# Batch 2's queries and keys by a half-precision copy and transposed loads, with a new written order of the front

## The chip, the cores and the metric

The kernel runs on one core of a Trainium2 chip. The metric is the device time of one execution in microseconds (us), lower is better: the median of three runs. Beside it stands one profiled execution with its trace. PE is the matrix engine, DVE the vector engine, ACT the scalar engine, POOL and SP the two engines that issue nearly all DMAs here.

## The reference

Eight batches of twelve heads go through an attention whose softmax has one more term in its denominator; the result, head by head in a row, goes through two matrix products with a squared ReLU between them. In float32:

```python
batch, n_heads, seq, head_dim = (8, 12, 448, 64)
scores = scale * np.matmul(q, k.transpose(0, 1, 3, 2))
m = np.max(scores, axis=-1, keepdims=True)
e = np.exp(scores - m)
attn = e / (np.sum(e, axis=-1, keepdims=True) + np.exp(-m) + 1e-09)
attn_out = np.matmul(attn, v)
x = attn_out.transpose(0, 2, 1, 3).reshape(B * S, H * D)     # 3584 x 768
h = x @ w_in                                                 # 768 x 2048
r = np.maximum(h, 0.0)
out = (r * r) @ w_out                                        # 2048 x 768
```

## The kernel before

All matrix products run in half precision. The written order of steps is what each engine gets: `manual_schedule` is on, each engine and each DMA queue takes its steps in the order of the string, and an engine waits where data or a buffer is not there yet. A step is a letter with numbers. `ORDER` is the front, run once; `CYCLE` is run twice, for batches 4 and 5 and for batches 6 and 7 (`period(b)` with b = 4 and 6); then a plain loop does the last two batches of the two matrix products.

What the letters mean, as far as they are needed:

- `s` scores of 64 keys of a quad (four heads) into one of two PSUM buffers, `e` the exponential of them on ACT, `a` the sums on DVE, `S` `Z` `M` the denominator, `v` the products with the values (`p`, `b`, `y`, `z`, `n`, `x` are the like for batch 0, which is done in halves), `X` the division that writes a quad of the transposed attention output `xt`.
- `j` two or six of the six partial products of a tile (128 of 2048 columns) of the first layer, `k` the ReLU, `l` the square. In the front `j0` to `j15` are batch 1's tiles and `j16` to `j31` batch 0's; `i` is a pair of tiles of half of batch 0.
- `o` pieces of the second layer for 128 tokens and half the columns, `O` and `Q` its two steps out of PSUM; `Q` also issues the store on SP.
- `d` a load from the list `LOADS` (in `CYCLE`, of `following`).

There are two ways by which a batch's queries and keys get into the tile `qk` with the head dimension on the partitions. Batches in `ON_PE` (line 37) are loaded on POOL in natural layout as half precision (`load_quad`, tile `nn`), transposed by PE (`T`, 14 transposes for a quad's queries or keys) into PSUM, and copied to `qk` by DVE or ACT (`U`). The others are staged: POOL issues two DMAs that copy q and k to DRAM as half precision (`stage`), SP issues three DMA transposes of 128 x 2688 elements out of that copy (`transposed_load`: queries, keys, and keys shifted by one position), and POOL copies the last keys of each head into a tile of their own (`tail_keys`). The scores of a staged batch need all three planes. They are made by eight matmuls of 224 columns in place of four of 448, and the rows of the output then lie in the store in steps of 2 and not of 7.

`qk`, the value tile `vn` and the tail keys have two buffers each, so batch b waits for batch b-2 to be done with them. The tile `ot` of a finished output piece has five buffers; one comes free when its store has landed. DMAs that POOL issues are in one hardware queue (q0 of the profile), those that SP issues in another (q1). Of each kind at most eight are under way, since each waits for the one eight before it.

In the front before the change, batches 0, 1 and 2 are transposed by PE and only batch 3 is staged; batch 4 is staged there too. The weights `win` (four loads of two DMAs) and `wout` (four DMAs) come in on the same POOL queue.

Of the kernel before, what the change touches and what calls it, by code (L numbers as in the profile page):

```python
# [16 lines left out]
def kernel(  # L17
# [17 lines left out]
    NQ = H // 4  # L35
    KC = S // 64
    ON_PE = (0, 1, 2)
# [21 lines left out]
    osb_pool = ctx.enter_context(tc.tile_pool(name="osb", bufs=5))  # L59
# [103 lines left out]
    def transposed_load(b, i):  # L163
        qk = qk_of(b)
        n, x, c = PLANES[i]
        nc.sync.dma_start(
            out=qk[:, i, 0:c],
            in_=stages[n, b][x:x + c * 2 * D].rearrange("(r c) -> r c", c=2 * D),
            transpose=True,
        )  # L170
# [501 lines left out]
    def other_ring():  # L672
# [4 lines left out]
        d0 W8 d8 d1 c1,4,0 c0,0,1 t0,0,0 c1,0,1 t1,0,0 u0,0,0,0 t1,0,4 u1,0,0,0 c0,4,1 u1,0,4,1 t0,0,4 d2 s0 t0,1,0 u0,0,4,1 u0,1,0,0 t1,1,0 u1,1,0,0  # L677
        d10 d9 s1 t0,1,4 e0 t1,1,4 e1 s2 e2 u0,1,4,0 s12 e12 u1,1,4,0 T0,1,0 T0,1,1 U0,1,0,0,4,0 U0,1,1,0,4,0 U0,1,1,4,7,0 U0,1,0,4,7,0 s3 s4 p2 p0 e3
        b0,0 e4 s6 p1 d18 p3 s5 e6 e5 b0,1 b0,2 T0,2,0 b0,3 y0 T0,2,1 U0,2,0,0,4,0 z0 n0 U0,2,1,0,4,0 b1,0 s8 U0,2,0,4,7,0 U0,2,1,4,7,0 x0 d3 d17 d16
        b1,1 s9 d15 T1,0,1 e8 e9 U1,0,1,0,7,0 T1,0,0 U1,0,0,0,7,0 b2,0 s11 e11 s10 s13 e10 e13 s14 p8 b2,1 p4 d5 b2,2 p9 s7 e14 p10 b2,3 p11 y2 p5 e7  # L680
        z2 b1,2 p6 s15 b1,3 p7 e15 y1 b3,0 n2 x2 b3,1 z1 s17 e17 b3,2 p12 p13 b3,3 n1 s18 p14 s16 e18 p15 x1 y3 T1,1,0 U1,1,0,0,7,0 e16 b4,0 z3 b4,1
        s19 e19 i0,6 n3 r0,6,0 s20 e20 s21 i0,7 s22 x3 b4,2 e21 p16 b4,3 e22 b5,0 r0,7,0 p17 p18 p19 d4 b5,1 g0,6 y4 z4 n4 s23 T1,1,1 e23 d13 s27 b5,2
        x4 i0,4 s28 p20 p21 g0,7 b5,3 e27 p22 p23 y5 U1,1,1,0,7,0 e28 z5 r0,4,0 n5 x5 s26 s29 e26 j20,0,2 j23,0,2 j23,2,4 j20,2,4 j20,4,6 e29 j23,4,6
        s25 k23,1 s24 g0,4 e25 e24 k20,0 P0 i1,7 j19,0,2 l23 a0,0 s32 e32 a0,1 s36 d6 j19,2,4 e36 j16,0,2 l20 j19,4,6 j17,0,2 s34 s33 k19,1 r1,7,0
# [4 lines left out]
        v1,0 v1,1 v1,2 v1,3 v1,4 d23 v1,5 k26,1 v1,6 a2,0 a2,1 a2,2 s44 s47 M1 l26 e44 j21,2,4 d22 j21,4,6 i1,4 X1 a2,3 k21,1 v2,0 v2,1 v2,2 r1,4,0 S2
        e47 v2,3 Z2 v2,4 v2,5 l21 v2,6 M2 o0,0,4 s46 o0,4,8 d14 s50 e46 e50 o0,8,12 X2 o0,12,16 s51 g1,4 s48 O0,1 Q0 j15,0,2 j0,0,2 j15,2,4 j4,0,2  # L690
        j15,4,6 j4,2,4 j4,4,6 j0,2,4 e51 e48 j0,4,6 s45 k15,1 l15 o2,0,4 s49 e45 e49 o2,4,8 s52 d21 o2,8,12 a3,0 e52 o2,12,16 k4,1 k0,0 s53 a3,1 s55
        d24 j10,0,2 O2,1 j1,0,2 Q2 j10,2,4 j1,2,4 j10,4,6 l0 j14,0,2 l4 j1,4,6 j11,0,2 e55 k10,0 j14,2,4 a3,2 j11,2,4 k1,1 j8,0,2 l10 j14,4,6 j11,4,6
# [4 lines left out]
        j13,4,6 l5 a5,2 j3,0,2 j3,2,4 j3,4,6 k12,0 a5,3 s69 l12 k6,1 o3,0,4 l6 k13,1 k3,1 l3 S5 l13 o3,4,8 o3,8,12 o3,12,16 O3,0 Q3 e69 s70 Z5 s71 d26
        M5 v5,0 v5,1 v5,2 v5,3 e70 e71 v5,4 v5,5 v5,6 o9,0,2 o9,2,4 X5 o9,4,6 o9,6,8 s66 o9,8,10 s68 o9,10,12 o9,12,14 o9,14,16 e66 O9,0 o6,0,2 e68
        s67 s72 o6,2,4 o6,4,6 o6,6,8 e67 o6,8,10 Q9 a6,0 a6,1 e72 a6,2 s73 o8,0,2 o6,10,12 o6,12,14 o8,2,4 o6,14,16 s75 e73 O6,0 o8,4,6 o8,6,8 e75 s78
        Q6 o8,8,10 o8,10,12 a6,3 e78 o8,12,14 s79 o8,14,16 s77 v6,0 v6,1 v6,2 v6,3 e79 e77 v6,4 S6 v6,5 v6,6 Z6 M6 s74 O8,0 Q8 o7,0,2 o7,2,4 e74 X6  # L700
        o7,4,6 s76 e76 a7,0 o7,6,8 o7,8,10 o7,10,12 o7,12,14 a7,1 o7,14,16 s82 d28 o10,0,2 O7,1 o10,2,4 o10,4,6 Q7 o10,6,8 s80 a7,2 e82 o10,8,10
        o10,10,12 o10,12,14 o10,14,16 e80 s85 s83 o11,0,2 o11,2,4 e85 o11,4,6 o11,6,8 d31 O10,1 Q10 e83 s81 a7,3 d29 o11,8,10 o11,10,12 o11,12,14 e81
        o11,14,16 O11,1 Q11 s84 o12,0,2 s86 o12,2,4 o12,4,6 e84 e86 o12,6,8 o12,8,10 a8,0 o12,10,12 o12,12,14 o12,14,16 S7 a8,1 O12,0 o13,0,4 o13,4,8
        d30 o13,8,12 Z7 Q12 a8,2 o13,12,16 v7,0 v7,1 v7,2 v7,3 O13,1 v7,4 a8,3 v7,5 v7,6 M7 S8 Q13 v8,0 v8,1 Z8 v8,2 v8,3 M8 v8,4 v8,5 X7 v8,6 X8
# [7 lines left out]
    def period(b):  # L712
# [3 lines left out]
        def following(n):  # L716
            ahead, what = ((1, n) if n < 6 else (2, 6) if n < 7 else (1, 6) if n < 8 else (2, n - 8))
            t = b + ahead
            if t < B and (n != 7 or b > FIRST_PERIOD):
                if what < 3:  # L720
                    transposed_load(t, what)
                elif what < 5:
                    tail_keys(t, (what - 2,))
                elif what == 5:
                    load_v_quads(t)
                else:
                    stage(t)
# [98 lines left out]
```

## Time and profile before

| what | value |
|---|---|
| time, median of 3 runs (all three) | 392.37 us (391.68 to 394.08) |
| the profiled execution, its own time | 392.36 us |
| its span in the profile | 390.6 us |
| instructions | 14257 |
| DMA packets | 75052, 45.34 MB |
| POOL's queue q0 | 24752 packets, 22.62 MB, 37.6% of 16 engines' span |
| SP's queue q1 | 49952 packets, 21.59 MB, 28.6% |
| transposed loads of queries, 5 | median 6.2 us from issue to landing |
| transposed loads of keys, 10 | median 7.1 us |
| loads of `wout`, 4 of 768 KB | median 15.3 us |
| copies of q to DRAM, 4 of 676 KB | median 14.0 us |

Lines of the profile are read as follows. A group of instructions has its line in the kernel, engine, operation, output and inputs, shape and count; then its busy time, the mean duration of one in ns, and the engine's idle time before it with what ended it. Lines 93 and 254 are helpers (`mm` and `exp`), so the tiles tell the steps apart. The duration of one matmul has its latency in it, and up to four matmuls run side by side in quarters of the array, so a busy PE need not be a full one. `DMA` in tenths is the mean busy share of the 16 DMA engines.

### The profile page before, as it was taken

The page shows a single profiled execution, that of the slowest core. Times are in us where ns is not written, and L with a number is a line of the kernel's source. Part 1 is how long each engine was busy: PE and PEld are TensorE (multiplying, and loading weights), DVE is VectorE, ACT ScalarE, POOL GpSimd, SP SyncE. Part 2 cuts the span into 40 slices and gives each one's busy share as a digit, 9 for nine tenths or more (in the row PEclk, how much of TensorE's full clock was granted, in tenths as well). Part 3 has the DMA queues.
Part 4 walks back from the last instruction along what each step waited for, and adds up shares of the span by engine and source line. Part 5 has one row for each costly group of instructions (what it writes and reads, how often), then busy time and mean ns, then how long its engine had stood idle before and what let it go on. Part 6 is the DMA issues. An engine that isn't in the chain of part 4 may idle for free.

```text
span 390.6 us, 14257 instructions
## 1 busy us (share of the span) xinstructions
PE 381.8 (98%) x6432; PEld 254.3 (65%) x6432; DVE 253.5 (65%) x468; ACT 228.3 (58%) x308; POOL 61.9 (16%) x96
## 2 busy tenths in 40 slices
PE   9689999999999999999999999999999999999997
PEld 5566656565689865567777665567777755556665
DVE  3887995765765766556968757575878788880000
ACT  5999998586689611249989731248988720001221
POOL 8443420025000700410001240210000000000000
PEclk9999999999999999999999999999999999999999
DMA  8999999999939899903129697901112200001132
GB/s 144 204 204 205 201 199 206 159 203 176 215 84 166 168 186 118 201 2 66 44 59 196 148 178 156 165 4 44 60 48 64 64 23 2 0 0 62 61 82 81
DMA packets 75052, 45.34 MB, mean 116 GB/s; under 512 B 47472, under 2 KB 72944, under 8 KB 74992
## 3 DMA queue, kind: packets, MB, share of 16 engines
q0 software_dynamic: 24752, 22.62, 37.6%
q1 hardware_dynamic: 49952, 21.59, 28.6%
q8 instruction: 50, 0.82, 1.0%
q10 hardware_dynamic: 288, 0.23, 0.2%
q14 instruction: 10, 0.08, 0.1%
HBM read 45.69 MB, written 17.93 MB: 163 GB/s over the span
## 4 chain that ended last, share of the span: by engine, by line
PE 89%; ACT 5%; DMA 2%; DVE 2%; POOL 1%; issue 1%; POOLq 0%; DVEq 0%; ACTq 0%
PE mp L93 79%; PE sp L93 8%; ACT et L254 3%; DMA nn<-in_k_dram 2%; PE mp L207 1%; POOL nn L117 1%; ACT rcp L372 1%; ACT rcp L365 0%; DVE half L441 0%; DVE xt L487 0%; DVE half L443 0%; DVE half L445 0%; ACT rcp L466 0%; ACT rcp L463 0%; DVE half L447 0%
## 5 line engine op out<-in xcount | busy, mean ns | idle before, releaser
L93 PE MATMUL mp<-wout,gs 64*64 64x384 f16 (+2 forms) x2928 | 165.4, 322 | 0.0
L93 PE MATMUL mp<-xt,win 128*64 128x448 f16 (+2 forms) x1188 | 148.3, 347 | 0.1
L93 PEld LDWEIGHTS <-gs 64*64 64x64 f16 (+1 forms) x2928 | 103.8, 106 | 33.9
L93 PEld LDWEIGHTS <-win 128*64 128x64 f16 (+1 forms) x1188 | 83.2, 106 | 63.5 <-issue 4.2
L254 ACT ACTIVATE et<-sp 128x896 f16<-128x896 f32 (+2 forms) x131 | 110.6, 891 | 12.7 <-PE sp L93 12.2
L505 DVE TENSOR_SCALAR rt<-mp 128x448 f16<-128x448 f32 x87 | 54.0, 622 | 15.9 <-PE mp L93 12.9
L509 DVE TENSOR_TENSOR gs<-rt 128x448 f16<-128x448 f16 x128 | 49.4, 404 | 21.9 <-ACT rt L503 20.0
L503 ACT ACTIVATE rt<-mp 128x448 f16<-128x448 f32 x41 | 21.8, 543 | 64.9 <-PE mp L93 50.9
L575 ACT ACTIVATE ot<-mp 128x384 f32<-128x384 f32 (+2 forms) x31 | 14.9, 480 | 70.5 <-PE mp L93 70.4
L93 PE MATMUL sp<-qk 64*64 64x224 f16 (+1 forms) x1056 | 53.3, 274 | 1.9 <-ACT et L254 1.2
L93 PEld LDWEIGHTS <-qk 64*64 64x64 f16 x1056 | 32.8, 114 | 14.3 <-issue 5.7
L188 POOL COPY flatq<-qk 64x384 f16<-64x384 f16 x20 | 14.5, 724 | 169.6 <-DMA qk<-stage_k 169.1
L254 ACT ACTIVATE nn<-sp 128x896 f16<-128x896 f32 x42 | 37.1, 916 | 4.3 <-PE sp L93 4.2
L487 DVE TENSOR_TENSOR xt<-mp,rcp 128x448 f16<-128x448 f32 x42 | 24.3, 620 | 15.6 <-ACT rcp L466 10.0
L581 DVE SCALAR_TENSOR_TENSOR ot<-mp,ot 128x384 f32<-128x384 f32 x42 | 23.4, 557 | 14.0 <-ACT ot L575 11.5
L93 PEld LDWEIGHTS <-vn 64*64 64x64 f16 x756 | 22.5, 107 | 9.8 <-issue 1.4
L93 PE MATMUL mp<-et,vn 64*64 64x448 f16 (+1 forms) x448 | 24.5, 343 | 0.0
L577 DVE TENSOR_SCALAR ot<-mp 128x384 f32<-128x384 f32 x26 | 14.4, 555 | 15.1 <-PE mp L93 14.9
L463 ACT ACTIVATE rcp<-sp,one_b 128x896 f32<-128x896 f32 x21 | 21.1, 1007 | 3.3 <-PE sp L93 3.3
L466 ACT ACTIVATE rcp<-rcp 128x896 f32<-128x896 f32 x21 | 19.9, 949 | 0.5
L441 DVE TENSOR_TENSOR half<-et 128x1792 f16<-128x1792 f16 x15 | 16.5, 1100 | 4.3 <-ACT et L254 4.2
L443 DVE TENSOR_TENSOR half<-half,et 128x1792 f16<-128x1792 f16 x15 | 16.3, 1087 | 0.3
(59 smaller groups left out, 195.7 us busy)
## 6 DMA issues: line engine op xcount, KB each, us to landing
out_dram<-ot SPq DMA_DIRECT2D x52, 96.0 KB, 2.4
out_dram<-ot SPq DMA_DIRECT2D x19, 192.0 KB, 1.9
win<-in_moe_w_in_dram POOLq DMA_DIRECT2D x8, 384.0 KB, 12.3
wout<-in_moe_w_out_dram POOLq DMA_DIRECT2D x4, 768.0 KB, 15.3
vn<-in_v_dram POOLq DMA_DIRECT2D x10, 288.0 KB, 7.9
stage_q<-in_q_dram POOLq DMA_DIRECT2D x4, 676.0 KB, 14.0
stage_k<-in_k_dram POOLq DMA_DIRECT2D x4, 676.0 KB, 16.7
nn<-in_q_dram POOLq DMA_DIRECT2D x8, 224.0 KB, 8.9
```

Of the source, the lines that this page charges most:

```text
L93: return nc.tensor.matmul(out_, lhsT, rhs, start=start, stop=stop)
L254: nc.scalar.activation(out=out_, in_=in_, func=AF.Exp, scale=scale)
L441: nc.vector.tensor_add(esq[m], a[:, 0:w], a[:, w:2 * w])
L443: nc.vector.tensor_add(esq[m], esq[m], z[:, 0:w])
L463: nc.scalar.activation(out=rcp, in_=zp[:, :, 0:S], func=AF.Ln, bias=one_b)
L466: nc.scalar.activation(out=zqs[m], in_=zqs[m], func=AF.Exp, scale=-1.0)
L487: nc.vector.tensor_mul(xts[b][:, 2 * g + i, :], xqs[m][i][:, 0:S], zqs[m][:, i, :])
L503: nc.scalar.activation(out=rt[:, 0:m], in_=hp[:, 0:m], func=AF.Relu)
L505: nc.vector.tensor_scalar(out=rt[:, 0:m], in0=hp[:, 0:m], scalar1=0.0, scalar2=None, op0=ALU.max)
L509: nc.vector.tensor_mul(gs[:, f0:f0 + per, t0 % RING:t0 % RING + n], r, r)
L575: nc.scalar.activation(out=ot, in_=op[:, 0:w], func=AF.Copy, scale=OUT_SCALE)
L581: nc.vector.scalar_tensor_tensor(out=ot, in0=lo[:, 0:w], scalar=OUT_SCALE, in1=ot, op0=ALU.mult, op1=ALU.add)
```

## The change

Four things change. Batch 2 leaves `ON_PE`: its 84 transposes on PE and six copies out of PSUM go, and it is staged, loaded transposed, and its tail keys copied, as batch 3 is. The order string of the front is a new one: the first layer of batch 0 lies beside the attention of batch 1, then comes the first layer of batch 1 as a block, and then the attention of batches 2 and 3 beside the second layer. The loads move: in the front only batches 2 and 3 are staged; a cycle that begins with batch b stages and loads b and b+1, where before it loaded b+1 and b+2. And `ot` has eight buffers.

```diff
-    ON_PE = (0, 1, 2)
+    ON_PE = (0, 1)
...
-    osb_pool = ctx.enter_context(tc.tile_pool(name="osb", bufs=5))
+    osb_pool = ctx.enter_context(tc.tile_pool(name="osb", bufs=8))
...
-        x = {(0, 1): (0, 0), (0, 2): (0, 1), (1, 0): (1, 0), (1, 1): (0, 0), (1, 2): (0, 1),
-             (2, 0): (1, 0), (2, 1): (1, 1), (2, 2): (0, 0)}[b, g]
+        x = {(0, 1): (0, 0), (0, 2): (0, 1), (1, 0): (1, 0), (1, 1): (0, 0), (1, 2): (0, 1)}[b, g]
...
-    LOADS = ([lambda b=b, g=g: load_quad(b, g) for b in range(3) for g in range(NQ) if b + g]
+    LOADS = ([lambda b=b, g=g: load_quad(b, g) for b in range(2) for g in range(NQ) if b + g]
              + [lambda b=b, g=g: load_v_quads(b, g, g + 1) for b in range(2) for g in range(NQ)]
-             + [lambda: load_v_quads(2)]
              + [lambda i=i: load_win(i, NW) for i in range(NW)]
-             + [lambda n0=n0, y=y: load_wout(n0, y, 2) for n0 in (0, HALF) for y in range(2)]
-             + [lambda: stage(3), lambda: transposed_loads(3), lambda: tail_keys(3), lambda: load_v_quads(3),
-                lambda: stage(4), lambda: transposed_loads(4), lambda: tail_keys(4), lambda: load_v_quads(4), lambda: stage(5)])
+             + [lambda n0=n0, y=y: load_wout(n0, y, 2) for n0 in (0, HALF) for y in range(2)])
+    for b in (2, 3):
+        LOADS += [lambda b=b: stage(b), lambda b=b: load_v_quads(b)]
+        LOADS += [lambda b=b, i=i: transposed_load(b, i) for i in range(3)]
+        LOADS += [lambda b=b, i=i: tail_keys(b, (i,)) for i in (1, 2)]
...
-            ahead, what = ((1, n) if n < 6 else (2, 6) if n < 7 else (1, 6) if n < 8 else (2, n - 8))
-            t = b + ahead
-            if t < B and (n != 7 or b > FIRST_PERIOD):
+            t, what = (b + 1, n) if n < 7 else (b, 6) if n < 8 else (b, n - 8)
```

`ORDER` and `CYCLE` are new strings with the same steps, but for batch 2's `T` and `U` steps and the `d` steps. The place in the new `ORDER` that the prediction speaks of, with the numbers of `LOADS` (19 stages batch 2; 21, 23 and 22 are its transposed loads; 15 to 18 load `wout`; 26 stages batch 3, 20 and 27 load the values of batches 2 and 3; 28 to 30 are batch 3's transposed loads; `s45` is the first score of batch 2):

```
        ... s16 d11 b3,1 s19 z2 e16 b3,2 T1,0,1 s18 n2 e19 x2 s17 d19 e18 p12 e17 b3,3 ...
        ... T1,1,1 T1,1,0 U1,1,1,0,7,0 z5 n5 d21 s26 x5 e26 d18 s28 ... i1,6 d10 d23 ... d15 l22 ... d22 ... d16 ...
        v2,5 M2 X1 v2,6 X2 j27,0,2 j27,2,4 l26 j27,4,6 d17 j7,0,2 ... (batch 1's sixteen tiles) ... d26 ...
        j8,4,6 o0,0,2 s45 s48 o0,2,4 ... d20 ... O0,0 Q0 ... d27 ... d30 ... d28 O1,0 j10,0,2 d24 d25 d29 s51 Q1 ...
```

In the program that comes out of it, POOL issues its DMAs from the first of `win` on in this order: the eight of `win`, with four of batch 1's queries and keys and two of its values between them; the two copies of batch 2; one `wout`; the last values of batch 1; three `wout`; the two copies of batch 3; four DMAs of batch 2's values and four of batch 3's. SP issues the three transposed loads of batch 2 before the first store, and those of batch 3 behind it.

More of the change, by code (lines that the diff above doesn't have):

```diff
@@ L681 @@
[L681 to L684, printed above, removed]
@@ L689 @@
[L689 to L692, printed above, removed]
@@ L697 @@
[L697 to L704, printed above, removed]
+        d0 W8 c0,0,1 c1,4,0 c1,0,1 t0,0,0 c0,4,1 u0,0,0,0 t1,0,0 u1,0,0,0 t1,0,4 t0,0,4 s0 u0,0,4,0 u1,0,4,1 t0,1,0 u0,1,0,0 t1,1,0 u1,1,0,0 s1 e0
@@ new lines @@
+        t0,1,4 e1 s2 e2 t1,1,4 u0,1,4,0 u1,1,4,0 T0,1,0 s12 d5 d1 d2 T0,1,1 U0,1,0,0,4,0 e12 s3 e3 U0,1,1,0,4,0 s4 e4 p2 s5 b0,0 b0,1 e5 p0 p3 s15
+        b0,2 e15 U0,1,0,4,7,0 b0,3 p1 y0 U0,1,1,4,7,0 s6 T0,2,1 z0 b1,0 e6 d6 s7 U0,2,1,0,4,0 T0,2,0 U0,2,0,0,4,0 n0 s9 e7 U0,2,1,4,7,0 U0,2,0,4,7,0
+        s8 e9 b1,1 e8 T1,0,0 U1,0,0,0,7,0 s10 s13 b1,2 e10 p4 b1,3 p5 b2,0 d7 p6 p7 y1 d14 d13 b2,1 s11 d3 d12 e13 x0 e11 p8 s14 p9 z1 d8 d4 b3,0 n1
+        b2,2 e14 p10 b2,3 p11 d9 y2 x1 s16 d11 b3,1 s19 z2 e16 b3,2 T1,0,1 s18 n2 e19 x2 s17 d19 e18 p12 e17 b3,3 p13 p14 p15 y3 U1,0,1,0,7,0 b4,0 s21
@@ new lines @@
+        i0,7 z3 s20 b4,1 n3 i0,6 b4,2 e21 e20 x3 s22 r0,7,0 p16 p17 p18 b4,3 p19 y4 b5,0 e22 g0,7 r0,6,0 z4 n4 s23 s27 e23 i0,4 b5,1 s24 x4 p20 p21
+        b5,2 p22 p23 e27 b5,3 r0,4,0 e24 g0,6 y5 g0,4 T1,1,1 T1,1,0 U1,1,1,0,7,0 z5 n5 d21 s26 x5 e26 d18 s28 j20,0,2 j20,2,4 j20,4,6 U1,1,0,0,7,0 s29
+        e28 k20,0 l20 i1,6 d10 d23 e29 r1,6,0 s36 s25 e36 e25 j22,0,2 j22,2,4 j22,4,6 s30 k22,0 s32 P0 a0,0 T1,2,0 e30 T1,2,1 e32 s34 i1,7 g1,6 s33
+        a0,1 e34 U1,2,0,0,7,0 a0,2 e33 s31 e31 j16,0,2 j23,0,2 j23,2,4 j23,4,6 r1,7,1 s35 s37 e35 U1,2,1,0,7,0 j16,2,4 a0,3 g1,7 j16,4,6 d15 l22 v0,0
@@ new lines @@
+        j11,4,6 j15,4,6 k6,0 l6 j5,0,2 j5,2,4 j12,0,2 k11,0 j5,4,6 j12,2,4 k5,1 l11 l5 j2,0,2 j2,2,4 j2,4,6 k15,1 j12,4,6 j3,0,2 k2,0 j3,2,4 j3,4,6
+        j4,0,2 l15 l2 k12,1 j4,2,4 j4,4,6 j13,0,2 j1,0,2 j1,2,4 k3,1 l12 j13,2,4 j14,0,2 k4,0 j9,0,2 l4 j9,2,4 l3 j13,4,6 d26 j14,2,4 k13,1 j1,4,6 l13
+        k1,1 l1 j14,4,6 j0,0,2 k14,1 j0,2,4 j8,0,2 j9,4,6 j8,2,4 k9,0 j0,4,6 j8,4,6 o0,0,2 s45 s48 o0,2,4 l9 o0,4,6 l14 e45 o0,6,8 o0,8,10 o0,10,12
+        d20 o0,12,14 o0,14,16 k8,0 s47 e48 e47 s46 l8 k0,0 O0,0 Q0 o1,0,2 o1,2,4 o1,4,6 o1,6,8 o1,8,10 o2,0,2 s49 e46 e49 o1,10,12 s50 o1,12,14
@@ new lines @@
+        o1,14,16 o2,2,4 a3,0 s56 e50 o2,4,6 e56 d27 s55 o2,6,8 a3,1 e55 o2,8,10 a3,2 o2,10,12 s54 o2,12,14 d30 e54 s53 o2,14,16 d28 O1,0 j10,0,2 d24
+        d25 d29 s51 Q1 e53 e51 O2,0 j10,2,4 j10,4,6 s52 v3,0 v3,1 v3,2 v3,3 v3,4 a3,3 S3 k10,1 Q2 v3,5 e52 l0 Z3 l10 v3,6 a4,0 o5,0,2 o5,2,4 M3 s57
+        o5,4,6 o5,6,8 o5,8,10 e57 o5,10,12 s58 o5,12,14 o5,14,16 X3 a4,1 s65 O5,0 Q5 e58 o6,0,2 o6,2,4 e65 s63 o6,4,6 o6,6,8 s59 o6,8,10 e63 o6,10,12
+        e59 s62 o6,12,14 o6,14,16 s60 e62 e60 d31 o3,0,2 o3,2,4 s61 o3,4,6 e61 o3,6,8 s64 O6,0 e64 o3,8,10 a4,2 o3,10,12 Q6 a5,0 o3,12,14 o3,14,16
@@ new lines @@
+        a5,1 O3,1 Q3 a4,3 o4,0,2 o4,2,4 s69 s67 o4,4,6 o4,6,8 o4,8,10 e69 s68 a5,2 o4,10,12 o4,12,14 e67 e68 S4 v4,0 o4,14,16 v4,1 s66 v4,2 Z4 v4,3
+        a5,3 O4,0 v4,4 v4,5 M4 Q4 S5 e66 Z5 v4,6 M5 v5,0 X4 v5,1 v5,2 v5,3 a6,0 v5,4 v5,5 v5,6 s70 o7,0,2 o7,2,4 o7,4,6 o7,6,8 o7,8,10 d32 X5 o7,10,12
+        o7,12,14 s71 o7,14,16 O7,0 e70 s72 e71 o8,0,2 o8,2,4 o8,4,6 Q7 s75 e72 o8,6,8 s73 e75 a6,1 o8,8,10 a6,2 o9,0,2 o8,10,12 s74 o8,12,14 e73 s76
+        o9,2,4 o9,4,6 e74 e76 o8,14,16 O8,0 o9,6,8 s85 o9,8,10 Q8 s83 a6,3 o9,10,12 o9,12,14 o9,14,16 e85 e83 s81 o10,0,2 a7,0 s77 e81 O9,0 Q9 o10,2,4
@@ new lines @@
+        o10,4,6 o10,6,8 s79 o10,8,10 o12,0,2 e77 s78 o12,2,4 e79 o10,10,12 s80 e78 o12,4,6 o10,12,14 s84 o10,14,16 e80 o12,6,8 a7,1 O10,0 S6 o12,8,10
+        Q10 e84 o12,10,12 s82 e82 o12,12,14 a7,2 o11,0,2 o11,2,4 a7,3 o12,14,16 o11,4,6 o11,6,8 o11,8,10 o11,10,12 Z6 o11,12,14 o11,14,16 O12,1 a8,0
+        Q12 a8,1 v6,0 v6,1 s86 M6 v6,2 v6,3 v6,4 v6,5 v6,6 S7 O11,1 e86 Q11 v7,0 v7,1 v7,2 v7,3 Z7 M7 a8,2 X6 v7,4 v7,5 v7,6 o13,0,2 a8,3 o13,2,4
+        o13,4,6 o13,6,8 S8 o13,8,10 Z8 o13,10,12 X7 o13,12,14 o13,14,16 v8,0 O13,0 v8,1 v8,2 M8 v8,3 v8,4 v8,5 v8,6 Q13 X8
@@ L716, in following @@
         def following(n):
-            ahead, what = ((1, n) if n < 6 else (2, 6) if n < 7 else (1, 6) if n < 8 else (2, n - 8))
-            t = b + ahead
-            if t < B and (n != 7 or b > FIRST_PERIOD):
[L720 to L727, printed above, removed]
+            t, what = (b + 1, n) if n < 7 else (b, 6) if n < 8 else (b, n - 8)
+            if what < 3:
+                transposed_load(t, what)
+            elif what < 5:
+                tail_keys(t, (what - 2,))
+            elif what == 5:
+                load_v_quads(t)
+            else:
+                stage(t)
         def block(n):
@@ new lines @@
+        j7,4,6 d6 j4,0,2 k7,1 d7 d9 j4,2,4 l7 j5,0,2 j31,0,2 j31,2,4 j31,4,6 j20,4,6 d13 k20,0 l20 j4,4,6 k4,1 j5,2,4 j5,4,6 k5,1 d8 l4 j11,0,2
+        j26,0,2 j26,2,4 j11,2,4 l5 j11,4,6 j26,4,6 j28,0,2 j28,2,4 k11,1 j28,4,6 d10 k31,0 l11 j25,0,2 k26,1 s0,3 l31 s0,0 j25,2,4 k28,0 j1,0,2
+        j12,0,2 l26 j1,2,4 d12 j1,4,6 j6,0,2 l28 j25,4,6 j12,2,4 k1,1 j6,2,4 d1 k25,1 l1 j12,4,6 j6,4,6 k12,1 l25 j18,0,2 j18,2,4 j19,0,2 j19,2,4 k6,0
+        j18,4,6 l12 j24,0,2 j23,0,2 k18,1 j24,2,4 j24,4,6 l18 j19,4,6 l6 j23,2,4 k19,1 j23,4,6 j2,0,2 j2,2,4 l19 k24,0 l24 j2,4,6 j10,0,2 k23,0 l23
@@ new lines @@
+        j10,2,4 j8,0,2 j10,4,6 e0,3 k2,0 e0,0 j8,2,4 j8,4,6 d11 k8,1 l2 j29,0,2 j29,2,4 d2 j29,4,6 s0,1 d0 e0,1 k10,0 l8 l10 s0,5 k29,1 o0,0,2 o0,2,4
+        o0,4,6 o0,6,8 e0,5 o0,8,10 s0,2 o0,10,12 o0,12,14 o0,14,16 s1,4 O0,0 Q0 e0,2 o3,0,2 s0,6 a0,0 o3,2,4 o3,4,6 o3,6,8 e1,4 o3,8,10 e0,6 s2,1
+        o3,10,12 s0,4 o1,0,2 o3,12,14 e2,1 d5 o3,14,16 O3,0 Q3 o1,2,4 l29 s2,3 e0,4 o1,4,6 o1,6,8 o1,8,10 s1,1 o2,0,2 e2,3 o2,2,4 e1,1 s1,5 o1,10,12
+        e1,5 o1,12,14 s1,2 a0,1 e1,2 o2,4,6 o1,14,16 O1,1 a0,2 s1,0 e1,0 o2,6,8 o2,8,10 a0,3 s1,3 e1,3 Q1 o2,10,12 o2,12,14 o2,14,16 O2,0 Q2 v0,0 S0
@@ new lines @@
+        o7,14,16 o8,0,2 s4,3 O7,0 s4,2 o8,2,4 Q7 o8,4,6 e4,3 e4,2 o8,6,8 o8,8,10 s3,6 o8,10,12 e3,6 o8,12,14 s4,1 o8,14,16 o9,0,2 e4,1 a3,0 s4,0 e4,0
+        o9,2,4 O8,0 o9,4,6 Q8 a3,1 a3,2 s4,6 e4,6 o9,6,8 o9,8,10 s4,5 o10,0,2 a4,0 o9,10,12 s4,4 e4,5 o10,2,4 o9,12,14 s5,4 o10,4,6 a3,3 o10,6,8 e4,4
+        o9,14,16 e5,4 o10,8,10 O9,1 s5,1 a4,1 o10,10,12 Q9 o10,12,14 s5,0 e5,1 o10,14,16 o12,0,2 o12,2,4 O10,0 s5,5 e5,0 o12,4,6 o12,6,8 s5,2 o12,8,10
+        o12,10,12 o12,12,14 e5,5 Q10 S3 e5,2 o12,14,16 s5,3 O12,0 e5,3 o11,0,2 Q12 Z3 o11,2,4 o11,4,6 o11,6,8 o11,8,10 o11,10,12 o11,12,14 a4,2
```

46 lines of the change are left out of this document (13 added, 33 removed).

## The prediction

> **What bounds the kernel now.** The page first: is any engine full, and where is the queue of loads full?
>
> ```profile
> PE 381.8 (98%) x6432; PEld 254.3 (65%) x6432; DVE 253.5 (65%) x468; ACT 228.3 (58%) x308; POOL 61.9 (16%) x96
> ...
> DMA  8999999999939899903129697901112200001132
> ```
>
> PE is the bound, by its busy time in nearly every slice. The DMA engines are full for the first 100 us (a slice is 9.8 us) and half empty after 170. The chain of waits tells what PE's work costs when nothing holds it:
>
> ```profile
> 42.82 1.68 PE mp L207 x56
> ...
> 52.29 1.68 PE mp L207 x56
> ...
> 135.06 36.44 PE mp L93 x384
> ```
>
> Columns: start, length, what. 384 matmuls of 448 columns on half the array take 94.9 ns each, so a column on the whole array takes 0.4236 ns. With this price the written order gives PE's work up to any step: 116.7 us for the whole front before, 114.5 after (six `T` steps of 14 transposes, 0.38 us each, are gone); a cycle has the same work as before. By counting matmuls in the trace of before, PE had done the front at 134.5 us. So it lags 17.8 us behind its work there. At 65 us the lag is 16.4 already: it arises where loads and ACT hold the start. Stage by stage:
>
> ```profile
> 0.00:30.00 30.00, 24.79 (x516) 17.30 (x516) 20.55 (x50) 25.17 (x41) 17.75 (x30) 1.00 1.12 184
> 30.00:60.00 30.00, 29.81 (x408) 17.71 (x404) 26.03 (x49) 28.03 (x39) 10.57 (x14) 1.00 1.24 202
> 134.50:390.60 256.10, 253.27 (x4052) 166.18 (x4044) 158.27 (x288) 119.18 (x158) 20.23 (x33) 1.00 0.45 82
> ```
>
> (Stretch, length, busy time of PE, weight loads, DVE, ACT, POOL, then clock, DMA share, GB/s.) From 30 to 60 us ACT is 93% busy and the DMA engines take all they can, about 200 GB/s. What a later load meets there is the question of this change. SP's queue, and two views of the DMA queues cut to 71 to 74 us and 141 to 146 us, show it:
>
> ```profile
> 67.18 9.15 SPq L166 DMA_TRANSPOSE qk<-stage_q  x1
> ...
> 117.83 4.07 SPq L166 DMA_TRANSPOSE qk<-stage_q  x1
> 122.00 6.55 SPq L166 DMA_TRANSPOSE qk<-stage_k  x2
> ...
> 135.44 15.31 SPq L166 DMA_TRANSPOSE qk<-stage_k  x1
> ```
>
> ```profile
> q0 software_dynamic: 571, 0.43, 92.3%
> q1 hardware_dynamic: 563, 0.15, 34.8%
> ```
>
> ```profile
> q0 software_dynamic: 240, 0.70, 89.4%
> q1 hardware_dynamic: 238, 0.06, 16.3%
> ```
>
> With POOL's queue empty, three transposed loads land 12.8 us after the first issue (117.83 to 130.6, by the landings in the trace). With POOL's queue full, one alone takes 12.7 (issued at 67.18) or 20.9 us (at 135.44). The packet counts tell why: in both stretches q0 and q1 move equally many packets (571 and 563, 240 and 238). A transposed load has 2688 packets of 256 bytes; q0's have 768 (`wout`), 896 or 3328 bytes (copies to DRAM). So while q0 has work, a transposed load gets on by one packet for each of q0's. Alone it does about 1000 packets a us (1995 from 78 to 80 us).
>
> **The change part by part.**
>
> PE's transposes: 84 at 27 ns of array time (30 in the chain) are 2.3 us off PE, all on its path. Six copies (0.62 us on DVE, 0.93 on ACT) cost nothing today and give little. Batch 2's scores have twice the matmuls at half the columns: the same array time; the weight loads beside them are at 65%, so zero.
>
> The DMA ledger. Intervals between landings in the saturated stretch of before: 1.13 us for a quad's queries, keys or values, 1.9 for a `win` DMA, 3.8 for a `wout`, 3.4 for a copy to DRAM. In before, the first values of batch 1 land at 41.5 with everything of batch 0, `win` and batch 1's queries and keys. The new order has carried the same then, less two quads of batch 2 (2.3), and one more quad of values (1.1): 40.4. Batch 2's copies land at 43.8 (q) and 47.2 (k). SP issues the first transposed load at 43.8; `qk`'s buffer has been free since batch 0's last scores (some 30 us). Packets flow 1.2 us after an issue (238.28 to 239.5), from 45.
>
> What q0 still holds then: the rest of k's copy (150 packets), four `wout` (4096) and batch 1's last values (256), batch 3's copies (416), batch 2's and batch 3's values (1536 each, in short rows). POOL is far ahead with issuing, since eight may be under way. Three transposed loads are 8080 packets. One for one, each stretch takes its time alone plus as many packets at 1000 a us: `wout` and values 16.3 + 4.4, to 68.5 us with 4500 packets done; batch 3's copies 6.8 + 0.4, to 75.7 with 4900; batch 2's values 4.8 + 1.5 (their landings at 98.7 to 103.5), to 82 with 6450; batch 3's the same, to 88.3 with 7990. The third load lands at about 89 us.
>
> When does PE need it? `s45` waits for all three loads. Before it stand 60.1 us of work: warm-up and batch 0 12.2, ten `T` 3.8, `i` 6.8, 75 pieces of `j` 28.5, batch 1's attention 8.5, one `o` 0.3. With the lag of 16.4 of before PE is there at 76.5. It waits 12.5 us. Behind `s45` in PE's order stand all pieces of the second layer, which could run but are written later; ACT and DVE run dry. Bounds: no wait, if q1 were served first (45 + 12.8 = 58); 18 us, if each goes as the one at 135.44 and lands with the end of q0 at 89 and more.
>
> After the wait: PE's first matmuls of the run, from rest, take 0.43 us for 512 columns, where the price above gives 0.217, for about 4 us. If 12 us of rest do the same, that is 2 us more; bounds 0 and 2.5; I take 2, since the only row from rest shows it. [...]
>
> The rest of the front: 54.3 us of work from `s45` on, and the lag grows as from there in before (17.8 - 16.9 = 0.9). Batch 3's loads stand behind the first store in SP's queue, 3 us after `s45`; q0 is empty by then, so 12.8 us and a tail copy (0.65 us each): done 17 us after `s45`, needed 22 us after it (`s69`). Zero, with 5 us of cover.
>
> The cycles: staging b+1 and then b waits on POOL only behind batch 3's tail copies, 38 us before the front's end; four copies are 13.6 us. Batch 4's transposed loads follow the front's last store, 12.8 us, with cover of 23 us of first-layer tiles ahead of `s0,3`. Zero; if they met a full q0 as those issued from 135.44 to 156.71, which took 30 us, 7 us per cycle. The loads of before did as much beside the same work. The eight buffers let stores wait some 10 us behind batch 3's loads; zero. The earlier half of the front keeps ACT's work with less beside it (41.6 us of PE work up to batch 1's last `X`, 47.5 before); it may cost a us of lag, which the wait at `s45` swallows.
>
> Sum on the profile's clock: 89 + 2 + 54.3 + 0.9 = 146.2 for the front, where before had 134.5; the rest 256.1: span 402.3. The profiled execution took 1.8 us beyond its span, and stands at the median (392.36, 392.37): **404 us**.
>
> **The rivals.**
>
> *No wait, a small gain.* If the two queues share bytes and not packets, 2.07 MB at half of 200 GB/s take 21 us, the loads land at 66, PE comes at 76.5, and 2.3 us of transposes are the result: 390; with a us or two less lag, since the block of batch 1's tiles needs neither ACT nor loads, 388.5. It decides where q1 gets 1.7 packets for one of q0. For it: 147 to 150 us, 444 packets against 101. Against it: there some DMA engines had drained q0; in the full stretches it is one to one. [...] Chance 0.17: 0.08 faster by over 1%, 0.09 within.
>
> *A short wait.* One to one, but PE later or q0 drained unevenly, so that the loads come 1 to 7 us late: 391 to 397. Chance 0.15, two thirds of it within 1%.
>
> *The wait of the forecast*, 7 to 17 us: 397 to 410. Chance 0.60.
>
> *A second wait*: batch 3's loads or batch 4's find a full queue, 5 to 10 us more: over 410. For it: the cover of 5 us. Against: q0's list ends before. Chance 0.08.
>
> **How the numbers follow.** The forecast alone reaches from 397 to 410; with the short wait and half of the first rival the range is 388 to 410. A measurement of this kernel tells 1% from no change (the three runs spread by 0.6%). Faster by over 1% (under 388.4): 0.08. Within: 0.09 + 0.10 = 0.19. Slower (over 396.3): 0.05 + 0.60 + 0.08 = 0.73.
>
> **What would show it.** PE idle for some 12 us from about 76 us, its releaser a transposed load of batch 2; the slice of `PEclk` there below 9; q0 and q1 with equal packet counts from 48 to 68 us; PE's transposes on line 207 down from 224 to 140. Wrong it is if the third load lands before 76 us, if PE reaches `s45` over 85 us for another reason, or if the time is lost in the cycles.

## The result and the profile after

The changed kernel takes **415.63 us** (median of six runs, 414.71 to 416.41) where the kernel before takes 392.44 (six runs beside it): 1.0592 times as long, interval 1.0573 to 1.0611. The forecast was 404 us, range 388 to 410. The direction and the place were foreseen; the size was not. The profiled execution took 415.27 us, its span is 413.5.

The page of the changed kernel, with the lines that answer to those of before (PE's busy time, then tenths in 40 slices of 10.3 us):

```profile
PE 384.9 (93%) x6432; PEld 254.2 (61%) x6432; DVE 247.1 (60%) x458; ACT 231.9 (56%) x312; POOL 62.4 (15%) x99
...
PE   9689999507999889999999999999999999999997
...
PEclk9999999956999999999999999999999999999999
DMA  9999999991979926999426329960221210001222
```

PE is busy 93% of the span in place of 98%. There is a hole in the slices from 72 to 103 us and a shallow dent in those from 134 to 155; the clock dips in the hole and just behind it. SP's queue (issues: start, length, what) and the chain of waits around the hole (start, length, what) say what it is:

```profile
43.52 10.52 SPq L166 DMA_TRANSPOSE qk<-stage_q  x1
54.10 34.67 SPq L166 DMA_TRANSPOSE qk<-stage_k  x2
```

```profile
75.23 20.07 DMA qk<-stage_k
...
95.35 0.96 PE sp L93 x16
96.31 4.48 PE mp L93 x56
100.79 0.38 PE sp L93 x16
```

PE stops at 78.4 us at the first score of batch 2. The third transposed load of batch 2, issued at 75.23, lands at 95.31, 51.8 us after the first was issued; 0.04 us later PE goes on. What it does first is slow: 56 matmuls of the second layer take 4.48 us. By windows (stretch, length, busy time of PE, weight loads, DVE, ACT, POOL, clock, DMA share, GB/s) the clock is half there, and behind the front nearly all is as before:

```profile
95.40:100.60 5.20, 5.20 (x76) 3.24 (x80) 0.00 (x0) 1.73 (x2) 2.44 (x4) 0.50 0.01 3
100.70:104.00 3.30, 3.30 (x103) 2.54 (x99) 2.21 (x3) 2.35 (x3) 0.00 (x0) 1.00 0.19 39
...
156.94:413.50 256.56, 253.68 (x4051) 166.08 (x4048) 150.29 (x274) 126.00 (x171) 21.87 (x36) 1.00 0.45 86
```

The front ends at 156.94 us (counted by matmuls, as before), 22.4 later than the 134.5 of before. The rest takes 256.6 in place of 256.1. So the loss is in the front. PE's waits between 80 and 170 us (waited for: us in total, times, longest) add one thing that no step of the prediction held:

```profile
PE sp L93 <- DMA qk<-stage_k: 16.9, 1, 16.9
PE mp L93 <- issue: 2.7, 2, 1.4
PE sp L93 <- issue: 0.4, 1, 0.4
```

Three times, 3.1 us in all, PE stops for "issue": nothing that the profile shows holds it. The front after the wait can be compared over one stretch, from 85 to 110 us of PE's work, the dense mixture of scores and output pieces: it takes 29.3 us here, and 25.6 in the quietest of the kernels below: 3.7 us, the three stops and a little beside them.

### The profile page after: what moved, and what is told of

It is laid out like the page before. It is cut to its first block, busy times and chain, and to the rows that moved or that the text cites. A ratio compares the mean times of both kernels' runs of the same rounds, so it can differ in the third digit from the quotient of the medians.

```text
span 413.5 us, 14241 instructions
## 1 busy us (share of the span) xinstructions
PE 384.9 (93%) x6432; PEld 254.2 (61%) x6432; DVE 247.1 (60%) x458; ACT 231.9 (56%) x312; POOL 62.4 (15%) x99
## 4 chain that ended last, share of the span: by engine, by line
PE 82%; DMA 7%; SPq 5%; ACT 3%; issue 1%; POOL 1%; DVE 0%; POOLq 0%; ACTq 0%
PE mp L93 72%; PE sp L93 9%; SPq L166 5%; DMA qk<-stage_k 5%; ACT et L254 2%; DMA nn<-in_k_dram 2%; PE mp L207 1%; POOL nn L117 1%; PE xp L93 0%; POOL vn L105 0%; ACT rcp L368 0%; ACT rcp L372 0%; POOL flatk L130 0%; ACT rcp L365 0%; POOL flatq L130 0%
## 5 line engine op out<-in xcount | busy, mean ns | idle before, releaser
L93 PE MATMUL mp<-wout,gs 64*64 64x384 f16 (+2 forms) x2928 | 170.2, 326 | 2.7 <-issue 2.7
L93 PEld LDWEIGHTS <-gs 64*64 64x64 f16 (+1 forms) x2928 | 104.9, 107 | 37.7 <-issue 3.7
L93 PE MATMUL sp<-qk 64*64 64x224 f16 (+1 forms) x1116 | 55.6, 269 | 20.1 <-DMA qk<-stage_k 16.9
L503 ACT ACTIVATE rt<-mp 128x448 f16<-128x448 f32 x51 | 27.5, 544 | 61.7 <-PE mp L93 55.2
L505 DVE TENSOR_SCALAR rt<-mp 128x448 f16<-128x448 f32 x77 | 48.0, 623 | 17.7 <-PE mp L93 14.8
L93 PEld LDWEIGHTS <-qk 64*64 64x64 f16 x1116 | 35.9, 117 | 34.6 <-DMA qk<-stage_k 17.3
L575 ACT ACTIVATE ot<-mp 128x384 f32<-128x384 f32 (+2 forms) x28 | 13.4, 479 | 69.8 <-PE mp L93 69.7
L577 DVE TENSOR_SCALAR ot<-mp 128x384 f32<-128x384 f32 x29 | 16.1, 556 | 46.2 <-PE mp L93 45.9
L188 POOL COPY flatq<-qk 64x384 f16<-64x384 f16 x24 | 16.5, 686 | 114.7 <-DMA qk<-stage_k 113.6
L111 POOL DMA_DIRECT2D vn<-in_v_dram x24 | 15.6, 661 | 71.6 <-PE mp L93 34.9
L443 DVE TENSOR_TENSOR half<-half,et 128x1792 f16<-128x1792 f16 x15 | 16.3, 1085 | 4.7 <-ACT et L254 4.6
```

Source lines behind the costliest of these rows:

```text
L93: return nc.tensor.matmul(out_, lhsT, rhs, start=start, stop=stop)
L188: nc.gpsimd.tensor_copy(km[rows_].rearrange("p h (x o) -> p h x o", o=2)[:, :, :, odd], src[:, :, S // 2 - 32:S // 2])
L443: nc.vector.tensor_add(esq[m], esq[m], z[:, 0:w])
L503: nc.scalar.activation(out=rt[:, 0:m], in_=hp[:, 0:m], func=AF.Relu)
L505: nc.vector.tensor_scalar(out=rt[:, 0:m], in0=hp[:, 0:m], scalar1=0.0, scalar2=None, op0=ALU.max)
```

## The experiments

Eleven kernels, most in three rounds (six runs for the last version, ten for the one with the cycle alone). Every time is set beside runs of the kernel before on the same chip, 392.1 to 392.3 us. "The first score" is that of batch 2, where PE waits. "The dense stretch" is the one just named, with the same instructions in each kernel.

**Batch 2's loads freed of the queue.** POOL takes its steps in order, so a step that waits for the loads keeps what stands behind it out of the queue.

```diff
  POOL's order:
-  wout, copies of batch 3, values 2, values 3, tail keys 2, tail keys 3
+  wout, values 2, tail keys 2, copies of batch 3, tail keys 3, values 3
```

> POOL copies batch 2's tail keys, and so waits for its three transposed loads, before it issues batch 3's copies to DRAM; batch 3's values come behind batch 3's tail keys. Batch 2's values stay ahead. Theory (one packet for one while the other queue has work): in the changed kernel SP's queue had moved some 4000 packets of 8064 at 70 us, when the last wout packets go; then 1536 packets of values at 240 a us, to 76.5 us with 5540 packets, then nothing is left to share with and the remaining 2520 go at up to 1000 a us. The third load lands at 79 to 81 us; PE, there at 78.4 us, waits 1 to 3 us in place of 16.9 and its clock is not halved. Time 415.6 - 14 to 16 - 2.7 = 397 to 399, and 393 to 395 if the 4 us of stops between 130 and 150 us go as well. Rival (transposed loads need their 50 us whatever the other queue holds): third load at 95, wait 17 us, time 415 to 416. Rival (the wait only moves to batch 3's loads): no wait at the first score of batch 2, one of 10 us or more at the first score of batch 3, time 408 or more.

Measured 401.60 us, ratio 1.026 (1.0227 to 1.0294): 14 us of the 23 are gone. The chain of waits of this kernel, at the first score of batch 2 and then at that of batch 3:

```profile
69.12 10.99 DMA qk<-stage_k
...
80.16 0.59 PE sp L93 x14
80.75 2.27 PE mp L93 x49
...
100.11 6.44 DMA qk<-stage_k
...
106.59 0.96 PE sp L93 x15
```

The third load lands at 80.11, inside the forecast, and PE waits 0.3 us there. The next piece takes 2.27 us where it took 4.48, PE having rested for 0.3 us only. So the loads are not slow by themselves. Part of the second rival holds too: batch 3's copies now start at 83 us, its loads land at 106.55, and PE waits 2.8 us for them, with a half clock behind it (0.50 from 106.6 to 109.6 us). The dense stretch takes 28.6 us: the stops for issue stay.

**Work for PE during the wait.** The first of two kernels puts 84 matmuls on constants before the first score, the second 112.

```diff
- ... j8,4,6 o0,0,2 s45 s48 ...
+ ... j8,4,6 f84 o0,0,2 s45 s48 ...
```

> 84 matmuls of 448 columns on constants stand on PE directly ahead of the first score of batch 2 (16 us of work, thrown away), so that PE is busy while it waits. The loads are untouched. Theory (the half clock after the wait costs 2.7 us): the granted clock stays 1.00 from 78 us on, the front ends 2.7 us earlier, time 412.9 in place of 415.6. Rival (after the wait ACT or the loads set the pace, the half clock costs nothing): 415.6, within 1 us.

> The changed kernel with 112 thrown-away matmuls in place of 84 ahead of the first score of batch 2: 21.7 us of work from 77 to 78.4 us on, to 98.5 to 100, past the landing of the loads at 95 to 98. PE never rests. Theory (the slow start behind the wait is the clock): granted clock 1.00 throughout, and the 56 matmuls of output pieces behind the first 16 of batch 2's scores take 2.3 us in place of 4.5 in the changed kernel and 3.3 with 84. Rival (they wait for ACT or for data): 4 us or more again. The time itself, 415 to 418, is set by the thrown-away work.

The first missed: 416.16 us, no gain. The loads landed at 97.34 this time, the filling ended at 93.7, and PE rested 3.7 us after all. The second (418.01 us, one run) bridges the wait. The chain behind the first score, of the first and of the second:

```profile
98.34 3.28 PE mp L93 x45
```

```profile
100.68 2.27 PE mp L93 x56
```

The same 56 matmuls take 4.48, 3.28 and 2.27 us with 16.9, 3.7 and no us of rest ahead (the chain of the second case goes through 45 of them; all 56 are in its trace). In the last case the granted clock is 1.00 over this work, where it was 0.50 in the changed kernel. So the slow start is the clock. Over the first 2.8 us of work behind the wait it costs 2.6 us in the changed kernel, and 1.4 to 2.6 in the five kernels here that rest there for 3.7 us or more.

**The cycle alone.** The kernel before, with the new `CYCLE` and its loads only.

```diff
  (kernel before)
- CYCLE, following: of before;  ORDER: ... d28 ... d31 ... d29 ... d30 ...
+ CYCLE, following: of the change;  ORDER without the loads of batches 4 and 5
```

> The kernel before with only the cycle of the change: its own front, less the loads of batches 4 and 5, and the new cycle with its own loads. Theory (the change loses everything in the front): everything behind the front takes 256 to 257 us as in both kernels, time 392 to 393. Rival (the cycle's loads, which POOL issues while the front still runs, bring the stops of 1 to 1.5 us that the changed kernel has between 130 and 150 us): 395 to 397.

Measured 393.48 us, ratio 1.0037 (1.0027 to 1.0048). The window from the front's end to the end of the span:

```profile
134.74:391.30 256.56, 253.69 (x4049) 166.11 (x4048) 150.13 (x274) 126.71 (x172) 21.68 (x36) 1.00 0.45 86
```

256.56 us, to the hundredth what the changed kernel has there, against 256.10 before: half a us in this profiled run, which took 393.05. By the medians the new cycle and its loads cost more, 1.4 us (393.48 against 392.06), half a us above the forecast of 392 to 393; where the rest of the 1.4 lies is not shown. Either way nearly all of the 23 us is lost in the front.

**Batch 5's copies put off.** They move behind batch 4's tail keys, out of the dense stretch.

```diff
  following, on POOL:
- d6 (copies b+1)  d7 (copies b)  d13 (values b)  d12 d11 (tail keys b)
+ d7  d13  d12 d11  d6
```

> The changed kernel, but in the cycle the copies to DRAM of batch b+1 come behind batch b's tail keys on POOL, so that between 122 and 145 us four copies less one half, 1.4 of 2.8 MB, are left in POOL's queue; the third transposed load of batch b+1 moves with them. Theory (PE's stops of 0.6, 1.3 and 1.4 us for nothing that the profile shows, between 133 and 147 us, are instructions that come late because POOL's queue holds all DMA engines): they go or shrink, time 412 to 413.5. Rival (PE's own stream is too dense there): the stops stay, 415 to 416. The wait of 16.9 us stays either way.

Measured 412.47 us, inside the forecast. The dense stretch falls from 29.3 to 26.9 us. Of the 3.7 us between the two profiled executions, this is 2.4; the loads of batch 2 landing 0.9 us earlier and a shorter half clock (1.1) come ahead of all that the edit moves, so they are scatter; and 0.7 us lost beside batch 6's copies, which have moved along in the next turn of the cycle, goes against it.

**Nothing in the queue beside the dense stretch.** As the last, and POOL waits for output piece 12 before it issues anything for batches 4 and 5.

```diff
- ... O12,1 a8,0 ...
+ ... O12,1 G12 a8,0 ...
+ "G": lambda n: nc.gpsimd.tensor_copy(gate, ots[128 * (n // 2), HALF * (n % 2)][:, 0:1]),
```

> The changed kernel with batch 5's copies behind batch 4's tail keys, and a one-column copy on POOL ahead of batch 4's copies that waits for the output piece 12, so that POOL's queue carries nothing between 115 and 148 us; batch 4's values come later as well. The wait of 16.9 us stays. Theory (PE's stops for issue are instruction packets that come late on DMA engines filled by POOL's queue): of the 4.0 us that PE loses against its own best pace between 125 and 149 us in the changed kernel, and 1.6 with batch 5's copies alone put off, nothing is left; every instruction packet comes 3 to 5 us after the one before, no longer 6.2; time 410.5 to 412. Rival (the stream itself is too dense for the instruction queue): the stops stay at 1.6 us or more, 412 to 416. If batch 4's transposed loads then come too late for the first score of the cycle, PE waits there for them, up to 8 us, and the time says nothing; the trace does.

The time missed: 413.95 us (413.13 to 417.20). In the profiled run, the slowest of four, batch 2's loads landed at 99.2 us, 4 later than in the changed kernel with the same loads; 1.4 of this is a later first issue (44.87 us against 43.52), and for the rest the runs tell no reason. The question of this kernel is answered by its waits from 80 to 170 us, which are one line:

```profile
PE sp L93 <- DMA qk<-stage_k: 21.6, 1, 21.6
```

No stop for issue is left there, and the dense stretch takes 25.6 us, 3.7 less than in the changed kernel.

**All in one, with and without that hold.** Tail keys of batch 2 and copies of batch 3 interleaved, batch 3's queries loaded first.

```diff
  POOL's order:
-  wout, copies 3, values 2, values 3, tail keys 2, tail keys 3, copies 5, copies 4, values 4
+  wout, values 2, tail keys 2 (one plane), copies 3, tail keys 2 (other), tail keys 3,
+  values 3, [hold], copies 4, values 4, tail keys 4, copies 5
```

> All in one: POOL copies batch 2's second plane of tail keys, issues batch 3's copies to DRAM, then copies the first plane; batch 3's queries are the first of its transposed loads; batch 3's values behind its tail keys; batch 5's copies behind batch 4's tail keys; and the one-column copy on POOL ahead of batch 4's copies that waits for output piece 12. Theory: from 401.6 us with batch 2's loads alone freed, the second wait goes (2.8 us), the half clock behind it (2.6 us) and the stops for issue (3.1 us): 393 to 395, no PE wait over 1.5 us from 76 us to the front's end. Rival (batch 3's loads still come late): a wait of 2 to 4 us at the first score of batch 3, 397 to 400.

> As the one with everything, but without the copy on POOL that holds batch 4's copies back: they follow batch 3's values at once. Theory (late instruction packets): stops for issue of 1 to 2 us where batch 4's copies and the dense stretch of scores and output pieces meet, 1 to 2 us more than the one with everything. Rival (the stops have nothing to do with the loads): same time as it, within 0.5 us, and as many stops in both.

397.58 us (1.0135, 1.0118 to 1.0152) with the hold, 398.93 (1.0164, 1.0136 to 1.0192) without. PE's waits from 80 to 150 us, without it and then with it:

```profile
PE mp L93 <- issue: 2.4, 2, 1.3
PE sp L93 <- DMA qk<-stage_k: 1.2, 1, 1.2
PE sp L93 <- issue: 1.1, 2, 0.9
```

```profile
PE sp L93 <- DMA qk<-stage_k: 2.2, 1, 2.2
```

Same instructions, same data, and the stops for issue are there or not by what is in POOL's queue: 29.1 against 25.6 us for the dense stretch. That the stops go with POOL's queue is shown by this pair. The total misses the 393 to 395: PE still waits 2.2 us at the first score, and 1.7 more by the half clock behind so short a rest; and 1.5 us go in the cycle, with a stop of 1.3 us at 193 us. There batch 6's copies run beside scores and output pieces (issued at 182.3, landed at 194.0). What the hold saves in the front, 3 us, is half given back.

**Batch 2's loads ahead of `wout`.**

```diff
  POOL's order:
-  copies 2, wout, values 2, tail keys 2 (one plane), copies 3, tail keys 2 (other), ...
+  copies 2, tail keys 2, wout, values 2, copies 3, tail keys 3, values 3, [hold], copies 4, values 4, copies 5
```

Besides, SP issues batch 3's transposed loads ahead of the first store.

> POOL copies batch 2's tail keys, and so waits for its transposed loads, before it issues any of wout; then wout, batch 2's values and batch 3's copies; batch 3's transposed loads (queries first) ahead of the first store; batch 3's values behind its tail keys. The one-column copy on POOL that waits for output piece 12 stays; behind it come batch 4's copies and values, then batch 5's copies in the same stretch of the cycle's first-layer tiles, where in the version with everything they came 26 us later, beside scores and output pieces. Theory (one packet for one, so a load that meets an empty queue lands early): batch 2's three loads land at 59 to 62 us in place of 80, wout at 76 to 79, no wait at the first score of batch 2; batch 3's loads land at 100 to 103, where PE arrives at about 100: a wait of 0 to 3 us. The 1.5 us that the cycle lost at batch 5's copies go. Time 393.5 to 396.5 in place of 397.6. Rival (transposed loads take some 35 us whatever stands beside them): they land at 80 again, wout at 95 and later, and PE waits for wout, 405 or more.

(The 1.5 us that this expectation puts down to batch 5's copies stood beside batch 6's, as just said.) This is the plainest view of the mechanism. SP's queue of this kernel, and the DMA queues from 48 to 57 us, when only the transposed loads are under way, and from 62 to 76, when only POOL's are (packets, MB, share of 16 engines):

```profile
43.43 4.78 SPq L166 DMA_TRANSPOSE qk<-stage_q  x1
48.27 6.52 SPq L166 DMA_TRANSPOSE qk<-stage_k  x2
```

```profile
q1 hardware_dynamic: 7195, 1.82, 113.0%
...
q0 software_dynamic: 3731, 2.83, 130.9%
```

The three loads land at 57.14, 13.7 us after the first was issued, where they took 51.8 in the changed kernel: same instructions, same bytes, and from 48 us on an empty queue. `wout` is there at 77.58, PE waits neither at the first score nor (0.4 us apart) for batch 3, and the front ends at 135.1 us, as before the change. The total is 397.57 (1.0120, 1.0089 to 1.0150), above the forecast of 393.5 to 396.5: in the profiled run (399.24, the slowest of four) batch 4's loads now share the queue with batch 5's copies, land at 160.55, and PE waits 2.3 us for them and has the half clock behind it (0.50 from 161.6 to 163.6 us); a stop of 1.5 us follows at 214, beside batch 7's copies.

**And the cycle's loads in the order of the change.** Behind the hold: copies 5, copies 4, values 4.

> As the one with batch 2's loads ahead of wout, but with the cycle's loads in the changed kernel's own order: behind the one-column copy on POOL come batch 5's copies, batch 4's copies, batch 4's values. Theory: batch 4's copy of k lands at 142 to 143 us and its transposed loads meet only 1536 packets of values, so they land at 155 to 157, ahead of the first score of the cycle at 158; the 4.0 us lost there go, and so do the 1.5 us of a stop for issue at 214 us beside batch 7's copies, which now come earlier. 397.6 - 5.5 = 392.1, 391 to 393.5: level with the kernel before. Rival (batch 4's loads now come later than with its copies first): 396 to 400.

Measured 396.74 us (1.0109, 1.0085 to 1.0133), where 391 to 393.5 was expected. Batch 4's loads land at 158.38, PE waits 0.3 us, and the front ends at 134.8. But batch 7's and 6's copies now run beside the dense part of the cycle. PE's waits from 76 to 215 us:

```profile
PE mp L93 <- issue: 2.6, 2, 1.7
PE sp L93 <- issue: 0.4, 1, 0.4
PE sp L93 <- DMA qk<-stage_k: 0.3, 1, 0.3
```

Behind the front this kernel takes 260.2 us, where before had 256.1. What one place gains another pays. No version tried beats the kernel before.

**Five output buffers in place of eight.**

```diff
-    osb_pool = ctx.enter_context(tc.tile_pool(name="osb", bufs=8))
+    osb_pool = ctx.enter_context(tc.tile_pool(name="osb", bufs=5))
```

> The changed kernel with five buffers of finished output tiles in place of eight. Theory (the buffers matter little, but stores stand behind batch 3's transposed loads for 10 us, from 104 to 115): 415 to 417, at most 1.5 us more than with eight. Rival (without the buffers PE waits for stores behind batch 3's loads): 418 or more.

415.58 us (413.79 to 417.02) against 415.63: the buffers do nothing that can be measured.

## Why the prediction came out as it did

The front of the forecast and of the profiled run, term by term. The stops are the dense stretch's excess over the quietest kernel, and the measured rest of the front is what the other terms leave:

| term | predicted | measured |
|---|---|---|
| PE reaches the first score | 76.5 us | 78.4 us |
| batch 2's third load lands | 89 | 95.3 |
| wait | 12.5 | 16.9 |
| half clock behind it | 2 | 2.6 |
| stops for issue | none | 3.7 |
| rest of the front, work and lag | 55.2 | 55.3 |
| front | 146.2 | 156.9 |
| the rest | 256.1 | 256.6 |

The front came out 10.7 us longer than forecast: 6.3 by the landing, 3.7 by the stops, 0.6 by the half clock.

**The mechanism of the wait was right.** One packet for one holds to the packet: the queues of the changed kernel from 48 to 68 us.

```profile
q0 software_dynamic: 3457, 2.64, 90.0%
q1 hardware_dynamic: 3456, 0.88, 40.5%
```

The rival in which the queues share bytes is out by these two lines, and by the landing 13.7 us after the issue once the queue is empty. In the trace 3457 packets of mostly 768 bytes go with 3456 of 256, as in the kernel before 240 of 2.9 KB on the mean went with 238 of 256: in both stretches the queues get on equally in number of packets, not in bytes. By how many packets at a time they change the counts don't tell.

**The step that failed first is the price of a shared packet.** The prediction let each stretch take "its time alone plus as many packets at 1000 a us". Alone, POOL's queue moves 3731 packets in 14 us, 3.75 ns each, and SP's 7195 in 9 us, 1.25 ns on the mean with its starts; a pair should take 5.0 ns at most, if sharing itself cost nothing. It took 20 us for 3457 pairs, 5.8 ns, which gives the 4352 pairs of `wout` and values 25.2 us in place of 20.7. They were due at 68.5 us (the terms that the prediction names, 47.2, 0.15, 16.3 and 4.4, add up to 68.1), and the last landed at 75.93. Another 3 us come with what stands behind: in the six profiled runs with batch 3's copies of 3328 bytes there the last `wout` lands at 75.3 to 80.7 us, in the three with values there, the first experiment's among them, at 71.8 to 72.0. How the copies do this is not shown. The three later stretches took 6.5, 5.1 and 7.3 us where 7.2, 6.3 and 6.3 were forecast, so the whole delay arises in the first. A row in the prediction's own fences had the price of sharing: 571 and 563 packets in 3 us are 5.3 ns a pair, or 23 us for the stretch. It was read for the ratio only. (The 896-byte packets that the prediction puts to copies to DRAM are loads of queries, keys and values, as their counts tell; the copies go in 3328. The sum does not hang on it.)

**PE's arrival** was 1.9 us late. The prediction took over the lag of before and allowed "a us" for the new early half. As it said, the wait swallowed it; but once the wait is gone it keeps the front from being shorter. In the last two versions PE reaches the first score at 78.4 to 79 us and the front ends at 134.8 to 135.1, no sooner than the 134.5 of before, though PE has 2.3 us less to do. Why PE comes late is not shown. The rival "no wait, a small gain" with its 390 us came about in none of the versions in which the wait is gone: they miss it by this and by what their cycles lose.

**The half clock** was mis-sized by 0.6 us: 2 taken, 2.6 measured, just above the bound of 2.5. It came behind a rest of 2.2 us (clock 0.50 from 82 to 84 us in the kernel with everything, 1.7 us lost), and not behind rests of 1.2 and 0.3 us at the same score. In the traces its spells last 3.41, 17.07 or 23.89 us, one, five or seven times the same length, and PE comes back at different points of one (behind the rest of 2.2 us the spell began at 81.07 us, 1.1 after PE was back): so the loss of 1.4 to 2.6 us does not follow the length of the rest.

**The stops for issue** were in no step. Every one ends just after a packet of 16,384 bytes on queue q8, which the profile calls "instruction": by the traces' records, all 21 stops of 0.88 us or more behind 76 us, in the eleven kernels that have one, end 2.1 to 2.5 us after such a packet's start. In the changed kernel the packets at 137.95 and 144.15 us come ahead of the two longer stops (timeline of PE; in brackets the idle time and its releaser):

```profile
140.22 0.35 PE L93 MATMUL mp<-wout,gs 64*64 64x384 f16 x3 [1.25 <-issue]
...
146.42 0.84 PE L93 MATMUL mp<-wout,gs 64*64 64x384 f16 x16 [1.44 <-issue]
```

The stops also stand at fixed places of the program. Counting PE's recorded instructions (matmuls, weight loads and a few others), the three of the changed kernel come after 3778, 4034 and 4290 of them, 256 apart; and all 29 stops for issue that the profiles name behind 76 us, from 0.2 us up, in twelve kernels, come at this same place in 256, within one, also where 84 or 112 matmuls more stand ahead. In the changed kernel q8 moves 50 of its packets for PE's 12877 instructions, one for each 256 or so. The reading of these counts is that PE stops at the ends of blocks of instructions, since it has run out of them. Those packets come 6.2 us apart there, with POOL's queue at 90% of the 16 engines, and 4.4 to 5.2 us apart over the same work in the kernel whose queue is empty. That the stops go with the queue is shown; that they are a want of instructions is read from the counts and the packets; that the packets themselves stand behind POOL's on a DMA engine is a reading that fits, not shown. The change brought the two together: in the kernel before, POOL's queue carries nothing from 110 to 132 us, beside its dense stretch, and SP's, whose packets fill 81% of the 16 engines' time then, brings no stop.

**What was costed at nothing** was nothing in PE's waits: the transposes' copies, the doubled matmuls of the scores, batch 3's loads, the buffers. For batch 3's loads it was close: they were to be done 17 us after the first score, with 5 us of cover; they landed 23 us after it, at 118.4, and only since PE was slower too, there at about 121, did nothing wait. The cycle's loads were not quite nothing: 0.5 us in the profiled run (1.4 by the medians of the cycle alone), and indirectly the stops, as POOL issues the cycle's first copies at 122 us, in the front. The rival of a second wait did not occur in the changed kernel, but the first version that removed the wait had one.

**Open**: why the third load lands anywhere from 94.4 to 99.2 us in six profiled runs with the same loads ahead of it (51.1 to 54.3 us after the first one's issue), and what the extra ns of a shared pair is.

## What to carry to other kernels

A small-packet load that is issued into a full queue got on here by one packet for each of the other queue's (3456 for 3457), so its landing was set by what the other engine had queued more than by its own size (51.8 us for three loads, 13.7 with 9 us of an empty queue): give it an empty queue by letting the engine that fills the other queue wait for it, and price sharing by a row in which both queues run, not by adding the two alone. A gap is paid more than once: PE came out of 16.9 us of it with a clock of 0.50, and every later load can slide against the work it was laid beside (batch 3's landed 23 us after the first score, 17 forecast). When a bound engine stops for nothing that the profile names, count the instructions between its stops (256 here), and look for instruction packets and for what fills the DMA engines then.

## What had not been expected of the hardware

PE stopped for 0.2 to 1.7 us a time, by the reading above for want of instructions; in the changed kernel in work of some 26 short matmuls a us (261 from 120 to 130 us), with POOL's queue at 91 to 95% of the 16 engines (131 to 137.9 us). In the kernel that keeps that queue empty beside the dense stretch no stop is left there; in the changed kernel the stretch takes 3.7 us more. And a rest of only 2.2 us cost 1.7 us by the half clock, as much as one of 16.7 us in another run (1.5).
